# Storing each output tile by one DMA of 128 partitions in place of two of 64 (pooled attention, then a gated feed-forward layer)

## The chip, the core and the metric

The kernel runs on one core of a Trainium2 chip. The metric is the device time of one execution in microseconds (us). The engines are PE (TensorE), DVE (VectorE), ACT (ScalarE), POOL (GpSimd) and SP (SyncE), which only issues DMAs; a core has 16 DMA engines, which all queues share.

## The reference

Eight batches, eight heads, 576 positions, head size 64. Keys and values are averaged over runs of eight positions, so each head attends to 72 keys. The result, 512 wide, goes through a feed-forward layer with a convolution over three positions as gate.

```python
k_p = k.reshape(B, H, 72, 8, 64).mean(axis=3)
v_p = v.reshape(B, H, 72, 8, 64).mean(axis=3)
attn = softmax(q @ k_p^T / 8)
x = (attn @ v_p).transpose(0, 2, 1, 3).reshape(8, 576, 512)
h = relu(x @ w_in)                        # 512 -> 1024
gate = sigmoid(conv_w[0]*h[s-1] + conv_w[1]*h[s] + conv_w[2]*h[s+1])
out = (h * gate) @ w_out                  # 1024 -> 512, float32
```

## The kernel before, in words

The batches go in four pairs, the groups g = 0 to 3. The 1152 positions of a pair are cut into nine tiles t of 128 rows. A position s of a batch is written as s = 9p + c, with p from 0 to 63 and c from 0 to 8; a tile holds two blocks, and a block is the 64 rows p of one c of one batch. Tile 4 of a group holds the last block of its first batch and the first block of its second; each other tile holds two neighbouring values of c. That makes 36 output tiles.

For each tile of attention PE makes scores, DVE and ACT the softmax, and PE the values. From the third group on (`TURN_DMA = 2`) the softmax weights `e` are turned into `eT`, and the attention's result `x` into `xT`, by transposing DMAs on SP's queue (`att_send`, line 703, and `att_turn_out`, line 756); two larger ones turn `q` into `qT` (line 555). The feed-forward layer works a batch at a time: w_in (line 777), ReLU on ACT (line 786), the convolution on PE or on DVE (lines 941 and 913), the product with the gate on DVE (line 991).

The output of a tile: `ffn_out` (line 999) multiplies with w_out into a PSUM bank, `ffn_copy` (line 1010) copies the bank on ACT or DVE into a tile in SBUF of 128 partitions with 512 float32 each, and `ffn_store` (line 1022) writes it to the result, a row of 2 KB from each partition. Rows of a block lie nine rows (18,432 bytes) apart in the result. The SBUF tiles come from a ring of five, `osb`; the nine tiles of the last group come from a ring of their own of eleven, `late`, which is laid over old buffers and so has the names `qp` and `v` in the profile. A later writer of a buffer waits until the store that reads it has landed.

All stores of the first three groups are issued by SP, in one queue with the transposes; those of the last group by SP or ACT. The very last tile is made in two halves of 256 columns, each with its own copy and its own stores. The input loads are issued by POOL, but for the first ones.

The order of all instructions is written out in `ORDER`, a list of operations with the engine of each, and `PLACES`, the PSUM banks. An operation of that list may issue more than one instruction: the store of a tile is one operation that issues two DMAs, but for the last tile, where each of the four stores is an operation of its own (`only` says which block). The DMAs of SP and ACT count on eight semaphores in turn, so that one waits for the landing of the one that had its semaphore before.

Of the kernel before, what the change touches and what calls it, by code (L numbers as in the profile page):

```python
# [12 lines left out]
ACT = mybir.ActivationFunctionType  # L13
# [20 lines left out]
class Graph:  # L34
# [121 lines left out]
    def add(self, engines, key, emit, after=(), behind=(), uses=(), mode=None, land=None, count=10):  # L156
        o = Op(engines, key, emit, uses, mode, land, count)
        for a, started in [(x, False) for x in after] + [(x, True) for x in behind]:
            if a is not None:
                a.next.append((o, started))  # L160
                o.left += 1
        self.ops.append(o)
        return o
# [20 lines left out]
def kernel(  # L184
# [10 lines left out]
    nc = tc.nc  # L195
# [4 lines left out]
    d_model, d_ff = moe_w_in.shape  # L200
    P = 128
    C = 9
    TB = S // C
# [59 lines left out]
    def buf(*key):  # L263
        return buffers[key[0]][tokens[key].slots[0]]
# [728 lines left out]
    def half_columns(x):  # L993
        return slice(x * d_model // 2, (x + 1) * d_model // 2)

    def ffn_out(g, t, fbs, ps, columns=slice(0, d_model)):
        rows = P
        for fb in fbs:
            nc.tensor.matmul(  # L999
                out=bank(ps)[0:rows, columns],  # L1000
                lhsT=buf("gT", g)[:, fb, t * P:t * P + rows],
                rhs=w_out_sb[:, fb, columns],
                start=(fb == 0),
                stop=(fb == n_fb - 1),
            )

    def ffn_copy(g, t, ps, copy, columns=slice(0, d_model)):
        rows = P
        osb = buf("late" if g == 3 else "osb", g, t)
        copy(out=osb[0:rows, columns], in_=bank(ps)[0:rows, columns])  # L1010

    def ffn_store(g, t, queue, only=None, columns=slice(0, d_model)):
        osb = buf("late" if g == 3 else "osb", g, t)
        if t == 4:
            blocks = [(groups[g][0], C - 1), (groups[g][1], 0)]
        elif t < 4:
            blocks = [(groups[g][0], 2 * t), (groups[g][0], 2 * t + 1)]
        else:
            blocks = [(groups[g][1], 2 * t - 9), (groups[g][1], 2 * t - 8)]
        for j, (b, c) in enumerate(blocks):  # L1020
            if only in (None, j):
                queue.dma_start(
                    out=out[b].rearrange("(p c) d -> c p d", c=C)[c, :, columns],
                    in_=osb[j * TB:(j + 1) * TB, columns],
                )

    def pe(*columns):
        return {"PE": sum(n / 2400 + 0.0025 for n in columns)}  # L1030
# [7 lines left out]
    def either(d, a):  # L1038
        return {"DVE": d - 0.085, "ACT": a - 0.085}

    def copier(o):
        return nc.scalar.copy if o.engine == "ACT" else nc.vector.tensor_copy

    def token(ring, *key, n=1):
        t = tokens[(ring,) + key] = Token(ring, n)
        return t
# [11 lines left out]
    def nudge(kind, b):  # L1058
        return 0.0
# [49 lines left out]
    for n in range(Graph.SPARES):  # L1109
        t = token("ps")  # L1110
# [299 lines left out]
    def add_out(b, w):  # L1410
        w += nudge("o", b)
        g, i = where[b]
        rounds = (1, 3, 5, 6, 7)
        for n, t in enumerate(n_outs[b]):
            key = w + 3 * rounds[n] - 1 + Graph.OUT + (Graph.LAST if b == B - 2 else 0) if b < B - 1 else w + n
            key += nudge("ot", 9 * g + t)
            osb, free = (token("late", g, t), [x for n in range(4, B) for x in qdone[n, 0] + [vdone[n]]]) if g == 3 else (token("osb", g, t), [])
            need = [a for x in groups[g][0:i + 1] for a in gdone[x]]
            if b == B - 1 and n == len(n_outs[b]) - 1:
                o = None  # L1420
                for x in range(2):
                    sm = token("ps")
                    o = add(pe(*[P * 2] * 8), key + x, lambda t=t, x=x, sm=sm: ffn_out(g, t, range(n_fb), sm, half_columns(x)),
                            after=need + [wout, o], uses=[sm, gtok[g]], mode=FULL, count=16)
                    c = add(either(0.42, 0.38), key + x, None, after=[o] + free, uses=[osb, sm])
                    c.emit = lambda c=c, t=t, x=x, sm=sm: ffn_copy(g, t, sm, copier(c), half_columns(x))
                    for r in range(2):
                        c2 = add({"SP": 0.7, "ACT": 0.6}, key + x, None, after=[c], uses=[osb], land=(2.4, 0, 1))
                        c2.emit = lambda c2=c2, t=t, x=x, r=r: ffn_store(
                            g, t, nc.scalar if c2.engine == "ACT" else nc.sync, r, half_columns(x))  # L1430
                continue
            sm = token("ps")
            o = None
            for j in range(2):
                o = add(pe(*[512] * 4), key, lambda t=t, j=j, sm=sm: ffn_out(g, t, range(4 * j, 4 * j + 4), sm), after=need + [wout, o],
                        uses=[sm, gtok[g]], mode=FULL, count=8)
            o = add(either(0.69, 0.585), key, None, after=[o] + free, uses=[osb, sm])
            o.emit = lambda o=o, t=t, sm=sm: ffn_copy(g, t, sm, copier(o))
            o = add({"SP": 1.36, "ACT": 1.16} if g == 3 else {"SP": 1.36}, key, None, after=[o], uses=[osb], land=(2.4, 0, 1))
            o.emit = lambda o=o, t=t: ffn_store(g, t, nc.scalar if o.engine == "ACT" else nc.sync)  # L1440
# [10 lines left out]
    for b in range(B):  # L1451
        g, i = where[b]
        w = b * SLOTS
        add_ffn(b, w)
        if b + 1 < B:
            ng, ni = where[b + 1]
            ts = n_tiles[b + 1]
            gap = Graph.SPREAD / len(ts)
            for n, t in enumerate(ts):
                add_att(ng, t, w + Graph.ATT + n * gap)  # L1460
        add_out(b, w + SLOTS)
# [39 lines left out]
```

## Time and profile before

| what | value |
|---|---|
| time, median of 3 runs | 210.96 us (210.22 to 211.09) |
| the profiled execution's own time | 211.08 us |
| its span, first to last instruction | 209.2 us |
| mean granted TensorE clock | 0.993 |
| DMA: packets, bytes | 48,835 packets, 33.48 MB |
| HBM written | 9.44 MB, the whole result |

The span is what the views of the profile divide up; the profiled execution's own time is 1.9 us longer. A view of the DMA in a stretch of time gives the mean busy share of the 16 DMA engines in forty slices, the GB/s that they moved, and for each queue its packets and the time that these took, as a share of 16 engines over that stretch. Queue q0 is POOL's, q1 is SP's, q10 is ACT's. A row of data makes a packet of its size, and packets of 4 bytes mark the end of a DMA on each engine that worked on it.

### The profile page before, as it was taken

To read this page: it belongs to the slowest core of one execution; us is meant where nothing else is said; L and a number is where in the kernel's file an instruction comes from. 1 tells how busy PE (TensorE), PEld (TensorE's weight loads), DVE (VectorE), ACT (ScalarE), POOL (GpSimd) and SP (SyncE) were. 2 spreads that over 40 slices of the span, in tenths; PEclk is the share of its full clock that TensorE was granted. 3 is DMA by queue.
4 is the path that set the end of the run, shared out by engine and by line. 5 is a ranking of instruction groups with operands and counts; after the bars stand their busy time and mean duration, and the time that the engine had idled before them with its cause. 6 is when DMAs were issued, how large, how long until landed. Compare 5 with 4: busy or idle time off the path is not lost.

```text
span 209.2 us, 6541 instructions
## 1 busy us (share of the span) xinstructions
PE 197.5 (94%) x2650; PEld 134.5 (64%) x2666; DVE 190.2 (91%) x338; ACT 174.5 (83%) x363; POOL 45.4 (22%) x74
## 2 busy tenths in 40 slices
PE   4899999999999999999999999999999999999990
PEld 1468688776688887666867875566556666644450
DVE  7969999889999999999999999999999999999440
ACT  3558786998899999998998999999999999797310
POOL 8553034010173121010000152040234306000000
PEclk9999999999999999999999999999999999999997
DMA  5999999999999999998495975895665557044496
GB/s 189 251 204 207 207 207 208 210 205 205 189 151 195 207 209 206 179 155 169 89 147 97 120 126 122 110 134 130 137 138 123 116 126 174 0 100 102 107 270 179
DMA packets 48835, 33.48 MB, mean 160 GB/s; under 512 B 28300, under 2 KB 43812, under 8 KB 48804
## 3 DMA queue, kind: packets, MB, share of 16 engines
q0 software_dynamic: 15216, 15.40, 44.8%
q1 hardware_dynamic: 32592, 16.20, 38.7%
q10 hardware_dynamic: 996, 1.45, 2.8%
q8 instruction: 21, 0.34, 0.6%
q14 instruction: 10, 0.08, 0.2%
HBM read 32.52 MB, written 9.44 MB: 201 GB/s over the span
## 4 chain that ended last, share of the span: by engine, by line
PE 50%; DVE 24%; ACT 15%; issue 5%; DMA 3%; SPq 0%; DVEq 0%; ACTq 0%
PE psum L777 21%; PE psum L999 12%; DVE tg L913 6%; DVE negm L635 4%; ACT x L740 4%; PE psum L719 3%; DMA hT<-in_k_dram 3%; DVE gT L991 3%; DVE sd L647 3%; PE psum L941 2%; PE psum L694 2%; PE psum L609 2%; ACT hT L786 2%; ACT qT L561 2%; PE psum L764 1%
## 5 line engine op out<-in xcount | busy, mean ns | idle before, releaser
L777 PE MATMUL psum<-xT,w_in_sb 128*128 128x288 bf16 x512 | 70.6, 286 | 0.4
L999 PE MATMUL psum<-w_out_sb,gT 128*128 128x512 bf16 (+1 forms) x280 | 65.9, 373 | 1.1 <-issue 0.2
L777 PEld LDWEIGHTS <-w_in_sb 128*128 128x128 bf16 x512 | 48.3, 98 | 15.6 <-issue 0.6
L786 ACT ACTIVATE hT<-psum 128x576 bf16<-128x576 f32 x64 | 41.6, 671 | 4.8 <-PE psum L777 4.2
L999 PEld LDWEIGHTS <-gT 128*128 128x128 bf16 x296 | 27.7, 98 | 27.5 <-DVE gT L991 0.6
L861 POOL COPY hT<-hT 128x126 bf16<-128x126 bf16 x14 | 11.3, 809 | 84.2 <-issue 43.6
L913 DVE SCALAR_TENSOR_TENSOR tg<-hT,ratio 128x576 f32<-128x576 bf16 x36 | 28.2, 811 | 0.5 <-ACT gT L923 0.2
L635 DVE TENSOR_REDUCE negm<-psum 128x8 f32<-128x576 f32 (+2 forms) x37 | 27.3, 747 | 1.3 <-PE psum L609 0.7
L913 DVE SCALAR_TENSOR_TENSOR tg<-hT,ratio,tg 128x576 f32<-128x576 bf16 x36 | 28.1, 807 | 0.0
L923 ACT ACTIVATE gT<-tg,ratio 128x576 bf16<-128x576 f32 x36 | 27.3, 792 | 0.8 <-DVE tg L913 0.7
L991 DVE TENSOR_TENSOR gT<-gT,hT 128x2304 bf16<-128x2304 bf16 x16 | 21.4, 1348 | 0.1
L740 ACT ACTIVATE x<-psum,r 128x64 bf16<-128x64 f32 x96 | 21.2, 357 | 0.1
L1010 ACT COPY osb<-psum 128x512 f32<-128x512 f32 x27 | 16.4, 620 | 4.3 <-PE psum L999 2.7
L647 DVE TENSOR_TENSOR sd<-psum,negm 128x576 f32<-128x576 f32 x27 | 19.7, 745 | 0.1
L684 ACT ACTIVATE e<-sd 128x576 bf16<-128x576 f32 x27 | 19.4, 719 | 0.1
L719 PE MATMUL psum<-vm,eT 128*128 128x65 bf16 (+5 forms) x240 | 18.8, 222 | 0.2 <-DVE vm L517 0.2
L719 PEld LDWEIGHTS <-eT 128*128 128x128 bf16 (+1 forms) x240 | 14.8, 101 | 3.6 <-issue 0.8
L747 DVE TENSOR_TENSOR x<-psum,r 128x512 bf16<-128x512 f32 (+1 forms) x25 | 16.6, 678 | 0.2
L426 PE MATMUL psum<-gT 128*128 128x448 bf16 x40 | 13.0, 433 | 2.8 <-DVE gT L1108 2.8
L941 PE MATMUL psum<-hT,dw 64*64 64x63 bf16 (+2 forms) x448 | 13.2, 255 | 0.2 <-ACT kT L506 0.2
L513 DVE TENSOR_TENSOR v<-v 128x1280 bf16<-128x1280 bf16 (+2 forms) x24 | 12.9, 538 | 0.2
L941 PEld LDWEIGHTS <-dw 64*64 64x64 bf16 x448 | 10.9, 107 | 2.1 <-issue 1.4
(95 smaller groups left out, 236.5 us busy)
## 6 DMA issues: line engine op xcount, KB each, us to landing
out_dram<-osb SPq DMA_DIRECT2D x54, 128.0 KB, 2.4
v<-in_v_dram POOLq DMA_DIRECT2D x8, 512.0 KB, 13.9
qp<-in_q_dram POOLq DMA_DIRECT2D x7, 576.0 KB, 13.3
kk<-in_k_dram POOLq DMA_DIRECT2D x3, 1152.0 KB, 14.4
out_dram<-qp ACTq DMA_DIRECT2D x10, 128.0 KB, 3.3
hT<-in_k_dram SPq DMA_DIRECT2D x2, 576.0 KB, 5.3
w_in_sb<-in_moe_w_in_dram POOLq DMA_DIRECT2D x2, 512.0 KB, 15.3
w_out_sb<-in_moe_w_out_dram POOLq DMA_DIRECT2D x1, 1024.0 KB, 17.9
```

The lines of the kernel that those rows point to most:

```text
L635: nc.vector.tensor_reduce(out=a["m"][0:rows], in_=a["s"][0:rows, :, 0:2 * KW].rearrange("p a (h s) -> p a h s", s=Sp), axis=AX.X, op=OP.ma ...
L647: nc.vector.tensor_tensor(out=a["d"][0:rows], in0=a["s"][0:rows, :, 0:2 * KW].rearrange("p a (h s) -> p a h s", s=Sp), in1=a["m"][0:rows]. ...
L684: nc.scalar.activation(out=dst, in_=src, func=ACT.Exp,)
L719: nc.tensor.matmul(out=a["o"][lo:hi, h // 4, (h % 4) * (D + 1):(h % 4 + x1 - x0) * (D + 1)], lhsT=a["eT"][:, j, lo:hi], rhs=buf("vm", b)[: ...
L740: nc.scalar.activation(out=a["x"][0:rows, n * D:(n + 1) * D], in_=ov[:, n // 4, n % 4, 0:D], func=ACT.Identity, scale=r[0:rows, n // 4, n ...
L777: nc.tensor.matmul(out=banks(ps)[:, j, 0:SC], lhsT=w_in_block(dc, fb), rhs=buf("xT", g)[:, dc, i * S + j * SC:i * S + (j + 1) * SC], start ...
L786: nc.scalar.activation(out=h_of(b)[:, fb].rearrange("p (a s) -> p a s", a=2), in_=banks(ps)[:, :, 0:SC], func=ACT.Relu, scale=1.0 if (b, f ...
L913: nc.vector.scalar_tensor_tensor(out=acc, in0=h, scalar=w, in1=acc if tap else mid, op0=OP.mult, op1=OP.add)
L923: nc.scalar.activation(out=gate, in_=acc_of(b, fb, ps), func=squash(b, fb), scale=ratio[:, 1, fb:fb + 1])
L941: nc.tensor.matmul(out=banks(pss[r ^ c])[c * D:(c + 1) * D, j, lo:hi], lhsT=dw[r * D:(r + 1) * D, tap * n_fb + fb, :], rhs=hT[r * D:(r + 1 ...
L991: nc.vector.tensor_tensor(out=gate, in0=gate, in1=h_of(b)[:, four], op=OP.mult)
L999: nc.tensor.matmul(out=bank(ps)[0:rows, columns], lhsT=buf("gT", g)[:, fb, t * P:t * P + rows], rhs=w_out_sb[:, fb, columns], start=(fb == 0),
```

## The change

`ffn_store` issues one DMA for a whole tile. Its source is all 128 partitions of the tile in SBUF. Its target is an access pattern put together by hand over the two blocks: the outermost dimension counts the two blocks, with the distance between them as step, the next one the 64 rows of a block, the last one the columns. In the last tile the operation for the first block of a half now stores both blocks, and that for the second issues nothing.

```diff
-    def ffn_store(g, t, queue, only=None, columns=slice(0, d_model)):
+    def ffn_store(g, t, queue, columns=slice(0, d_model)):
         osb = buf("late" if g == 3 else "osb", g, t)
...
-        for j, (b, c) in enumerate(blocks):
-            if only in (None, j):
-                queue.dma_start(
-                    out=out[b].rearrange("(p c) d -> c p d", c=C)[c, :, columns],
-                    in_=osb[j * TB:(j + 1) * TB, columns],
-                )
+        b, c = blocks[0]
+        to = out[b].rearrange("(p c) d -> c p d", c=C)[c:c + 1, :, columns]
+        last = out[blocks[1][0]].rearrange("(p c) d -> c p d", c=C)[blocks[1][1]:blocks[1][1] + 1, :, columns]
+        step = last.offset - to.offset
+        to = bass.AP(tensor=to.tensor, offset=to.offset, ap=[[step, 2], *[list(x) for x in to.ap[1:]]])
+        queue.dma_start(out=to, in_=osb[:, columns])
...
-                            g, t, nc.scalar if c2.engine == "ACT" else nc.sync, r, half_columns(x))
+                            g, t, nc.scalar if c2.engine == "ACT" else nc.sync, half_columns(x)) if r == 0 else None
```

The order of the instructions on PE, DVE and POOL stays as it was, and on SP and ACT each pair of stores becomes one at the place of the first. SP's queue, where the transposes of the third group begin, minus before and plus now; `eT`, `qT` and `xT` are targets of transposes, and the sizes are those of the target's access pattern:

```order
 L703 DMA_TRANSPOSE eT_106<-e_99 128x5x128
-L1022 DMA out_dram<-osb_123 64x512 x2
-L1022 DMA out_dram<-osb_124 64x512 x2
+L1025 DMA out_dram<-osb_123 2x64x512
+L1025 DMA out_dram<-osb_124 2x64x512
 L555 DMA_TRANSPOSE qT_79<-qp_76 128x18x128
-L1022 DMA out_dram<-osb_126 64x512 x2
+L1025 DMA out_dram<-osb_126 2x64x512
 L756 DMA_TRANSPOSE xT_114<-x_107 128x4x128
 L703 DMA_TRANSPOSE eT_104<-e_103 128x5x128
```

Nothing changes its place; four issues between the transposes into `eT` and into `qT` become two, and the leading count of the target goes from 64 to 2.

The end of ACT's queue, where the last tiles of the last group are copied out of PSUM (`qp_77`, `v_87` are buffers of `late`) and stored:

```order
 L1010 COPY qp_77<-psum 128x512
-L1022 DMA out_dram<-qp_77 64x512 x2
-L1022 DMA out_dram<-v_87 64x256 x2
-L1496 UNCONDITIONAL_BRANCH
+L1025 DMA out_dram<-qp_77 2x64x512
+L1025 DMA out_dram<-v_87 2x64x256
+L1494 UNCONDITIONAL_BRANCH
```

The last four issues of ACT become two. The two of `v_87` were the blocks of the last tile's second half.

## The prediction

> **What bounds the kernel now.** I read the page first: who is busy, how the DMA engines fare over time, and the chain that ended last.
>
> ```profile
> PE 197.5 (94%) x2650; PEld 134.5 (64%) x2666; DVE 190.2 (91%) x338; ACT 174.5 (83%) x363; POOL 45.4 (22%) x74
> DMA  5999999999999999998495975895665557044496
> PE 50%; DVE 24%; ACT 15%; issue 5%; DMA 3%; SPq 0%; DVEq 0%; ACTq 0%
> ```
>
> PE is busy for 94% of the span, and the chain runs through PE, DVE and ACT; DMA has 3% of it. So the kernel is bound by compute. But the DMA engines are full for the first 17 slices of 5.23 us, and half full after. Next I asked for busy time by stage, cut where SP's queue changes its work.
>
> ```profile
> 0.00:56.00 56.00, 51.57 (x956) 36.56 (x959) 49.44 (x114) 40.80 (x68) 17.14 (x30) 1.00 1.17 209
> 56.00:89.00 33.00, 32.76 (x574) 25.68 (x576) 32.43 (x60) 31.98 (x64) 9.36 (x18) 1.00 1.17 188
> 89.00:165.00 76.00, 74.89 (x928) 50.61 (x923) 75.39 (x123) 73.86 (x178) 14.16 (x22) 1.00 0.73 128
> 165.00:195.00 30.00, 29.69 (x176) 17.10 (x178) 29.81 (x39) 26.37 (x55) 4.71 (x4) 1.00 0.43 96
> 195.00:209.20 14.20, 8.62 (x48) 4.51 (x46) 3.16 (x6) 1.49 (x3) 0.00 (x0) 0.90 0.73 205
> ```
>
> The last two columns are the DMA share and GB/s: over 1 in the load stages (packets of one engine overlap there), then 0.73, 0.43, 0.73. The stores leave room, as long as all 16 engines carry them. When they are issued is in the timeline of SP's queue:
>
> ```profile
> 56.70 1.19 SPq L1022 DMA_DIRECT2D out_dram<-osb  x2
> 82.75 6.36 SPq L703 DMA_TRANSPOSE eT<-e  x3
> 89.15 3.00 SPq L1022 DMA_DIRECT2D out_dram<-osb  x4
> ...
> 164.36 4.93 SPq L756 DMA_TRANSPOSE xT<-x  x3
> 169.38 15.46 SPq L1022 DMA_DIRECT2D out_dram<-osb  x14
> ```
>
> One tile is stored at 56.7 us. The other 35 come from 89.15 us on, mixed with transposes until 169.3 us.
>
> **What the change removes.** The issues of line 1022, by the view of that line (min/median/max in ns):
>
> ```profile
> L1022 SPq DMA_DIRECT2D out_dram<-osb x54: 466/591/1724, 56.7 to 202.2; - x54
> L1022 ACTq DMA_DIRECT2D out_dram<-qp x10: 473/527/1108, 195.4 to 204.1; - x10
> L1022 SPq DMA_DIRECT2D out_dram<-qp x6: 467/620/929, 187.3 to 203.4; - x6
> L1022 SPq DMA_DIRECT2D out_dram<-v x2: 683/768/852, 204.3 to 205.1; - x2
> L1022 ACTq DMA_DIRECT2D out_dram<-v x2: 473/516/560, 205.4 to 206.0; - x2
> ```
>
> Of 74 issues 37 go. SP saves 31 of some 0.59 us, 18 us, and none of it is on the chain (SPq 0%). ACT saves 6 of 0.52 us, at the very end, where nothing computes any more. So the gain is bounded by the tail: below, under the rivals.
>
> **What it adds: fewer engines for each store.** How many engines share a DMA can be counted from its packets. Four stores alone, and the first 9 us with ACT's only load, of 24 rows:
>
> ```profile
> DMA packets 320, 0.52 MB, mean 131 GB/s; under 512 B 64, under 2 KB 64, under 8 KB 320
> q1 hardware_dynamic: 320, 0.52, 56.7%
> out_dram<-osb SPq DMA_DIRECT2D x4, 128.0 KB, 2.4
> ...
> q10 hardware_dynamic: 36, 0.01, 1.0%
> gT<-in_moe_conv_w_dram ACTq DMA_DIRECT2D x1, 12.0 KB
> ```
>
> Four stores (182.4 to 186.4 us) make 256 packets of data and 64 small ones: 16 end marks for each 64 rows. The load of 24 rows makes 36 packets: 24 of data and 12 marks. With 16 engines at hand it ran on 12, which divides 24 evenly. So the engines are given equal shares of a leading count: 16 for 64, 12 for 24. The new store leads with 128 in SBUF and with 2 in the result (the 2x64x512 of SP's new rows). No DMA of this trace has sides that lead with different counts. Either the count of the source decides, then it is 16 engines, or the two sides must be cut alike, then the 2 blocks can be shared by 2 engines at most. I take 2: an engine that walks one side must know where it stands on the other, and a cut of the 64 inner rows is not a cut of the leading count.
>
> [...]
>
> **Its price.** Each of two engines then moves 64 rows of 2 KB where each of 16 moved 8. The lone stores took 56.7% of 16 engines for 4 us, 36.3 us for 256 rows, so 142 ns a row with all 16 engines on the same 64 partitions. In the tail SP's and ACT's queues run together and rows go faster (196 to 207 us):
>
> ```profile
> DMA  0297998997998898999488997997999899999969
> GB/s 0 67 253 164 231 156 239 373 305 216 417 305 209 291 261 216 268 313 313 179 246 223 253 201 186 365 358 224 298 253 179 201 313 365 261 305 283 287 235 283
> DMA packets 1750, 2.78 MB, mean 252 GB/s; under 512 B 342, under 2 KB 468, under 8 KB 1748
> q10 hardware_dynamic: 858, 1.36, 49.9%
> q1 hardware_dynamic: 890, 1.39, 38.6%
> ```
>
> On average 252 GB/s at 88.5% busy, 17.8 GB/s an engine or 115 ns a row; in the best slices 365 and 417 GB/s, 22.8 and 26.1 an engine, or 90 and 79 ns. Two engines that have the path to themselves are nearest to the best slices: I take 84 ns, 5.4 us a tile, with 79 to 115 ns for the range and 142 as a rival. If packets of stores overlapped as those of loads do (1.17 busy), 84 would act as 72 ns, 4.6 us a tile: that is the low end.
>
> **What else those two engines carry.** The transposes use all 16. From 89 to 195 us:
>
> ```profile
> DMA packets 29069, 12.63 MB, mean 119 GB/s; under 512 B 25984, under 2 KB 25984, under 8 KB 29056
> xT<-x SPq DMA_TRANSPOSE x18, 2.5
> eT<-e SPq DMA_TRANSPOSE x16, 2.7
> ...
> q1 hardware_dynamic: 6688, 1.65, 73.7%
> ```
>
> 25,984 small packets are 1624 an engine (the stores' marks among them). The last row is 99 to 113 us, where SP issues transposes alone: 6688 packets took 73.7% of 16 engines for 14 us, 24.7 ns each. So an engine spends 1624 x 24.7 ns = 40 us on them. They are in one queue with the stores: a transpose behind a store now lands some 5 us later, and attention waits, then PE.
>
> **The sum.** On the two engines, from 89.15 us:
> 36 tiles x 5.4 us = 194.4 us (35 from there on, and one for the tile at 56.7 us, which pushes 5.4 us of loads behind it while the engines are full), 40 us for transposes, 1.8 us from the last row to landing (2.4 us less the 0.57 us that four rows take). Together 325.4 us, if the two engines never rest. They rest when SP, which works in order, waits for compute before a transpose. From 89 to 165 us it waited, in 18 rows of which these are the first and last:
>
> ```profile
> SPq L756 <- ACT osb L1010: 4.8, 4, 2.2
> ...
> SPq L703 <- PE psum L941: 0.3, 1, 0.3
> ```
>
> In all 34 us. Stores still under way cover much of that; I count a third, 11 us. The end: 336 us of span. After 169 us compute has 40 us left without a transpose, against 20 tiles or 108 us of stores, so compute no longer counts. With the 1.9 us by which the profiled execution (211.08) is longer than its span: 338 us. That execution is within 0.1% of the median, so nothing is corrected.
>
> **Rivals.**
> 1. All 16 engines still share a store (its 128 rows are cut). For it: 128 rows can be shared by 16 engines as evenly as 64. Against: the count of 12 above shows that equal parts of a count decide, and 2 is one of the counts. Then only the tail changes:
>
> ```profile
> 203.66 0.42 DVE L1010 COPY v<-psum 128x256 f32<-128x256 f32 x1 [0.45 <-PE psum L999]
> 203.59 1.12 ACTq L1022 DMA_DIRECT2D out_dram<-qp  x2
> 205.41 1.13 ACTq L1022 DMA_DIRECT2D out_dram<-v  x2
> ```
>
> The last copy ends at 204.1 us, its last store is issued at 206.0 (ACT is held up by its earlier stores). One issue less for each of the last two tiles on ACT is 0.5 to 1.1 us: 210.0 to 210.6 us, I take 210.2. It decides if the new stores show 16 marks each. [...]
>
> 2. Two engines, at 142 ns a row: 9.1 us a tile, 36 x 9.1 = 327.6, with 89.15, 40, 1.8, 11 and 1.9 us 471 us. For it: it is the price of most stores now. Against: the rows of the tail.
>
> 3. Two engines, and little of it seen, because compute goes on while stores fall behind: then the five `osb` buffers would have to hold. They hold 27 us of stores, and 81 us come between 89 and 165 us (15 tiles). The bandwidth bound stays in any case: low prices and transposes that overlap alike (34 us at 1.17) give 89.15 + 36 x 4.6 + 34 + 1.8 + 1.9 = 292 us.
>
> **How the numbers follow.** Two engines: 0.90, of it 0.80 for prices of 72 to 115 ns, 0.06 for the second rival and beyond, 0.04 for less than 285 us. The first rival: 0.10; with 0.5% (1.05 us), what a measurement of this kernel can tell from no change, that is 0.04 faster, 0.06 the same. At 115 ns: 36 x 7.4 + 89.15 + 40 + 1.8 + 11 + 1.9 = 410 us. The range 285 to 410 us holds 0.8. Slower by over 0.5%: 0.90.
>
> **What would show it.** Right: stores of 256 KB that land after some 7 us in place of 2.4; 37 x 2 end marks in place of 74 x 16, so 1110 fewer packets, 47,725; in the tail under 55 GB/s with a small DMA share; PE at about 60% of the span, waiting behind transposes and `osb`; SP's queue ending the chain by DMA. Wrong: 592 end marks (48,243 packets) and a tail as fast as now; or DMA rows near 142 ns. The weakest terms are the price of a row on two engines and the third of SP's waits.

## The result and the profile after

| | before | after |
|---|---|---|
| time, median | 210.88 us (210.22 to 211.09) | 326.95 us (326.27 to 327.43) |
| ratio | | 1.551 (95% interval 1.546 to 1.556) |
| span of the profiled execution | 209.2 us | 325.5 us |
| granted TensorE clock, mean | 0.993 | 0.84 |

The changed kernel takes 116 us more. The page of the profile after, in the lines that answer to those of before: busy time of the engines; granted clock and DMA share in forty slices of 8.1 us, and GB/s; packets; the chain that ended last, by engine and by line.

```profile
PE 213.7 (66%) x2650; PEld 139.7 (43%) x2666; DVE 191.4 (59%) x338; ACT 175.5 (54%) x363; POOL 40.1 (12%) x74
PEclk9999999999999899798699598589587869555555
DMA  7999999999998998869879959811111111111111
GB/s 235 193 208 206 210 205 201 170 205 208 142 79 62 110 159 61 109 76 81 94 64 66 110 64 77 52 30 53 51 45 36 51 54 51 51 51 51 51 51 39
DMA packets 47725, 33.48 MB, mean 103 GB/s; under 512 B 27190, under 2 KB 42702, under 8 KB 47694
...
DMA 45%; PE 16%; ACT 8%; SPq 5%; issue 5%; DVE 4%; ACTq 3%; DVEq 0%; POOLq 0%
DMA out_dram<-osb 17%; DMA eT<-e 10%; DMA v<-in_v_dram 9%; PE psum L777 5%; DMA qp<-in_q_dram 5%; PE psum L999 4%; DMA xT<-x 3%; SPq L1025 3%; ACTq L1025 3%; ACT x L740 2%; DMA hT<-in_k_dram 2%; PE psum L719 2%; ACT osb L1010 2%; SPq L756 1%; DVE negm L635 1%
```

No engine is full any more, and DMA, which had 3% of the chain, has 45%. In the last third the DMA engines show a share of 0.1 and 51 GB/s, but for a gap near 243 us: two engines of sixteen. The packets are 1110 fewer, so each of the 37 stores has 2 end marks where each of 74 had 16.

The eights and nines in the row of the DMA share before that are not sixteen engines at full work, since GB/s fell. The trace keeps start, duration and size of every packet. From 89.6 to 215.1 us the packets of 256 bytes, which are those of the transposes, took 58 ns in the mean, where the kernel before had 24; the median is 18 ns in both. So a part of them stood for long. The trace names no engine, so it isn't shown what they stood for; the likely reading is the part of their transpose on the two engines that stores held.

The timeline of SP's queue (start, duration, both in us) shows the two stages:

```profile
89.61 2.44 SPq L1025 DMA_DIRECT2D out_dram<-osb  x2
92.16 12.85 SPq L555 DMA_TRANSPOSE qT<-qp  x1
...
199.85 12.55 SPq L756 DMA_TRANSPOSE xT<-x  x3
215.12 30.10 SPq L1025 DMA_DIRECT2D out_dram<-osb  x7
...
296.85 9.98 SPq L1025 DMA_DIRECT2D out_dram<-v  x1
```

The stage with transposes, 89.15 to 169.3 us before, now ends at 212.4 us. The 20 tiles after it start at 215.1 us, where before they started at 169.4. Who waited, over the whole run (total, times, longest):

```profile
ACT osb L1010 <- DMA out_dram<-osb: 37.5, 8, 8.3
PEld L719 <- DMA eT<-e: 24.2, 6, 10.3
PE psum L719 <- DMA eT<-e: 22.2, 6, 10.0
PE psum L777 <- DMA xT<-x: 6.6, 1, 6.6
```

ACT waits for a free output buffer, PE for softmax weights that a transpose has still to turn. Both are behind stores. The waits for `eT` and `xT` all fall into the stage with transposes, and so do 9.8 of ACT's 37.5 us; the other 27.7 us come after it. Busy time of the engines over that stage and the rest, before and then after (the last three columns are granted clock, DMA share and GB/s):

```profile
89.15:169.30 80.15, 78.99 (x938) 53.07 (x932) 79.54 (x129) 77.88 (x190) 15.43 (x24) 1.00 0.71 126
169.30:209.20 39.90, 34.06 (x194) 19.00 (x195) 28.68 (x38) 23.68 (x44) 3.43 (x2) 0.96 0.53 136
...
89.60:215.10 125.50, 89.40 (x944) 56.88 (x940) 81.11 (x130) 78.94 (x190) 11.94 (x24) 0.86 0.89 83
215.10:325.50 110.40, 40.98 (x194) 20.89 (x195) 28.03 (x36) 23.48 (x44) 1.61 (x2) 0.68 0.13 48
```

The stage with transposes is 45 us longer, and PE, the first column of busy time, has 10 us more of work in it, at a granted clock of 0.86 in place of 1.00. No run tells what these 10 us by themselves cost. The DMA view of the stage without transposes (222 to 312 us) gives the price of a row:

```profile
DMA packets 2195, 4.45 MB, mean 49 GB/s; under 512 B 34, under 2 KB 34, under 8 KB 2192
q1 hardware_dynamic: 1605, 3.23, 9.4%
q10 hardware_dynamic: 587, 1.19, 3.4%
```

The two queues fill 12.8% of 16 engines, which is two engines (12.5%) and a little more, because packets overlap: by the packet records two were under way for 87.6% of these 90 us, three for 9.7%, and never more. 12.8% of 16 x 90 us, for 2158 rows, is 85 ns a row. By what was moved, 51 GB/s on two engines, a row comes every 80 ns.

### The profile page after: what moved, and what is told of

Read it like the earlier page. It is cut to its first block, busy times and chain, and to the rows that moved or that the text cites. A ratio compares the mean times of both kernels' runs of the same rounds, so it can differ in the third digit from the quotient of the medians.

```text
span 325.5 us, 6493 instructions
## 1 busy us (share of the span) xinstructions
PE 213.7 (66%) x2650; PEld 139.7 (43%) x2666; DVE 191.4 (59%) x338; ACT 175.5 (54%) x363; POOL 40.1 (12%) x74
## 4 chain that ended last, share of the span: by engine, by line
DMA 45%; PE 16%; ACT 8%; SPq 5%; issue 5%; DVE 4%; ACTq 3%; DVEq 0%; POOLq 0%
DMA out_dram<-osb 17%; DMA eT<-e 10%; DMA v<-in_v_dram 9%; PE psum L777 5%; DMA qp<-in_q_dram 5%; PE psum L999 4%; DMA xT<-x 3%; SPq L1025 3%; ACTq L1025 3%; ACT x L740 2%; DMA hT<-in_k_dram 2%; PE psum L719 2%; ACT osb L1010 2%; SPq L756 1%; DVE negm L635 1%
## 5 line engine op out<-in xcount | busy, mean ns | idle before, releaser
L777 PE MATMUL psum<-xT,w_in_sb 128*128 128x288 bf16 x512 | 76.8, 302 | 12.3 <-DMA xT<-x 6.6
L999 PE MATMUL psum<-w_out_sb,gT 128*128 128x512 bf16 (+1 forms) x280 | 74.8, 410 | 12.2 <-ACT osb L1010 5.7
L777 PEld LDWEIGHTS <-w_in_sb 128*128 128x128 bf16 x512 | 50.9, 103 | 31.2 <-issue 14.2
L999 PEld LDWEIGHTS <-gT 128*128 128x128 bf16 x296 | 29.9, 105 | 44.7 <-issue 16.4
L1010 ACT COPY osb<-psum 128x512 f32<-128x512 f32 x27 | 16.3, 603 | 42.4 <-DMA out_dram<-osb 37.5
L719 PE MATMUL psum<-vm,eT 128*128 128x65 bf16 (+5 forms) x240 | 19.8, 228 | 22.3 <-DMA eT<-e 22.2
L732 DVE RECIPROCAL r<-psum 128x8 f32<-128x8 f32 (+1 forms) x37 | 7.2, 200 | 32.7 <-PE psum L719 31.4
L861 POOL COPY hT<-hT 128x126 bf16<-128x126 bf16 x14 | 7.7, 546 | 134.1 <-issue 75.0
L941 PE MATMUL psum<-hT,dw 64*64 64x63 bf16 (+2 forms) x448 | 14.2, 263 | 5.9 <-ACT osb L1010 5.6
L941 PEld LDWEIGHTS <-dw 64*64 64x64 bf16 x448 | 11.6, 110 | 7.9 <-issue 7.1
L426 PE MATMUL psum<-gT 128*128 128x448 bf16 x40 | 12.0, 403 | 2.8 <-DVE gT L1106 2.8
## 6 DMA issues: line engine op xcount, KB each, us to landing
v<-in_v_dram POOLq DMA_DIRECT2D x8, 512.0 KB, 15.9
```

Source lines behind the costliest of these rows:

```text
L719: nc.tensor.matmul(out=a["o"][lo:hi, h // 4, (h % 4) * (D + 1):(h % 4 + x1 - x0) * (D + 1)], lhsT=a["eT"][:, j, lo:hi], rhs=buf("vm", b)[: ...
L777: nc.tensor.matmul(out=banks(ps)[:, j, 0:SC], lhsT=w_in_block(dc, fb), rhs=buf("xT", g)[:, dc, i * S + j * SC:i * S + (j + 1) * SC], start ...
L941: nc.tensor.matmul(out=banks(pss[r ^ c])[c * D:(c + 1) * D, j, lo:hi], lhsT=dw[r * D:(r + 1) * D, tap * n_fb + fb, :], rhs=hT[r * D:(r + 1 ...
L999: nc.tensor.matmul(out=bank(ps)[0:rows, columns], lhsT=buf("gT", g)[:, fb, t * P:t * P + rows], rhs=w_out_sb[:, fb, columns], start=(fb == 0),
```

## The experiments

The theory: the target's leading count sets how many engines share a store, and 36 tiles at 84 ns a row on the same two engines set the end. Rival A: one large DMA from a pattern of three levels is slow as such. Rival B: the time comes from transposes that land late, not from the amount on two engines. Experiments 1 to 4 write rows to other places of the result, so they measure and could not replace the kernel.

**1. Two DMAs, leading count 2.** The store of before, with the 64 rows of a block walked as 2 x 32.

```diff
-                queue.dma_start(
-                    out=out[b].rearrange("(p c) d -> c p d", c=C)[c, :, columns],
-                    in_=osb[j * TB:(j + 1) * TB, columns],
-                )
+                to = out[b].rearrange("(p c) d -> c p d", c=C)[c, :, columns]
+                step, (d, w) = to.ap[0][0], to.ap[1]
+                to = bass.AP(tensor=to.tensor, offset=to.offset, ap=[[step, 2], [2 * step, 32], [d, w]])
+                queue.dma_start(out=to, in_=osb[j * TB:(j + 1) * TB, columns])
```

> Two DMAs of 64 partitions a tile as before, but the target of each leads with a count of 2 (2x32x512; the rows of a block are written in another order). Theory (the leading count of the target sets how many engines share a store, and engines 0 and 1 then carry 64 rows a tile at 84 ns): as the changed kernel, 327 us, within 10, with 2 end marks for each of 74 stores (47,799 packets). Rival A (one DMA of 128 partitions from a pattern of three levels is slow as such): 211 us. Rival B (the time comes from transposes that land late, not from the amount on two engines): two stores of 32 rows an engine let transposes in between more often, 270 to 320 us.

Measured: 328.07 us (ratio 1.560, 1.555 to 1.565).

```profile
DMA packets 47799, 33.48 MB, mean 102 GB/s; under 512 B 27264, under 2 KB 42776, under 8 KB 47768
```

The number of end marks is that of two engines (2 for each of 74 stores); that they are engines 0 and 1 is not shown, since the trace names none. Two DMAs of 64 partitions are as slow as the one of 128 as soon as the target leads with 2, so rival A is out as far as it is the size of the DMA. The three levels of the pattern are still here; experiments 2 and 3 have three levels too, and are far faster, so these are not what costs. Out as well is the form of rival B that expected less than 320 us.

**2. Two DMAs, leading count 4.** The same edit with `[[step, 4], [4 * step, 16], [d, w]]`.

> Two DMAs of 64 partitions a tile, each with a target that leads with 4 (4x16x512; rows of a block in another order). Theory: four engines with 32 rows a tile at 84 ns, 2.7 us; 36 x 2.7 = 97 us with 29 to 40 us of transposes from 89 us on, 217 to 230 us with landing and the 1.9 us outside the span, and up to 10 more where SP waits: 217 to 240 us. Rival A: 211 us. Rival B (late transposes): half of the changed kernel's delay, about 269 us.

Measured: 250.24 us (ratio 1.190, 1.186 to 1.193), between the two. SP's queue at the end of the transposes:

```profile
178.14 5.49 SPq L756 DMA_TRANSPOSE xT<-x  x3
184.17 19.99 SPq L1025 DMA_DIRECT2D out_dram<-osb  x14
```

Here neither side was right alone. The stage with transposes ends at 183.6 us, 14 us later than before, though its stores and transposes are only 70 to 81 us of work for four engines in its 95 us (15 tiles at 2.7 us, and 29 to 40 us). That part is rival B: transposes behind stores land late. The other part is bandwidth: 20 tiles x 2.7 us from 184.2 us on is 238 us, where compute without a transpose needed 40 us. My expectation had counted all tiles from 89 us and so missed that the last 20 can't start before the transposes are through. With landing and the time outside the span that makes 242 us. The DMA share from 184.1 to 249 us shows where the other 8 us went:

```profile
DMA  2222222222012222222122222222222222222210
```

Four engines would be 0.25, and there are gaps. By the packet records the rows took 93 ns in the mean here, 5.4 us more than 84 ns over 20 tiles, and for 4.1 us before the last row no store moved. The longest gap, at 200.4 us, ends after a copy for which ACT had waited for a free buffer. Why a row took 93 ns isn't shown.

**3. Two DMAs, leading count 8.** The same with `[[step, 8], [8 * step, 8], [d, w]]`.

> Two DMAs of 64 partitions a tile, each with a target that leads with 8 (8x8x512; rows of a block in another order). Theory: eight engines with 16 rows a tile, 1.3 to 2.3 us; 36 x 2.3 + 40 us from 89 us on is at most 212 us, so the engines hardly bind and compute does: 210 to 215 us. Rival B (late transposes): a quarter of the delay, about 240 us.

Measured: 218.05 us (ratio 1.037, 1.034 to 1.039), 3 us above the expected range. The transposes end at 169.1 us, as before, so what is left is the tail:

```profile
196.83 9.36 ACTq L1025 DMA_DIRECT2D out_dram<-qp  x6
206.29 0.59 ACT L1010 COPY qp<-psum 128x512 f32<-128x512 f32 x1 [8.95 <-DMA out_dram<-qp]
```

The same stores in the timeline of the kernel before:

```profile
196.93 5.95 ACTq L1022 DMA_DIRECT2D out_dram<-qp  x6
```

ACT, which works in order, takes 9.4 us for six stores of the last group and the waits between them, where it took 5.95, and copies the next tile after them. The two queues from 196 to 216 us:

```profile
q10 hardware_dynamic: 864, 1.44, 24.9%
q1 hardware_dynamic: 864, 1.44, 21.9%
```

Together 46.8% of 16 engines is nearly all of eight (50%). So eight engines do bind the kernel, but only at its end.

**4. One DMA of 128 partitions into a target that leads with 128.**

```diff
-        b, c = blocks[0]
...
+        rows = out[groups[g][0]:groups[g][1] + 1].rearrange("b s d -> (b s) d").rearrange("(p c) d -> c p d", c=C)
+        to = rows[t, :, columns]
         queue.dma_start(out=to, in_=osb[:, columns])
```

> One DMA of 128 partitions a tile as in the change, but into 128 evenly spaced rows of the result, so that its target leads with 128 (128x512; the rows of a tile go to other places of the pair's two batches, each row of the result is written once). Theory: 16 engines, 16 end marks for each of 37 stores (48,243 packets), and what the merging of issues is worth by itself: 209.5 to 211.0 us. Rows read from all 128 partitions take nearer 84 than 142 ns. Rival A (one large DMA is slow as such): over 250 us.

Measured: 207.87 us against 210.56 (ratio 0.988, 0.987 to 0.990): faster by 2.7 us, more than expected. The page's packets, then two of its stores alone (181 to 186 us), then the end of the timeline:

```profile
DMA packets 48243, 33.48 MB, mean 162 GB/s; under 512 B 27708, under 2 KB 43220, under 8 KB 48212
...
DMA packets 288, 0.52 MB, mean 105 GB/s; under 512 B 32, under 2 KB 32, under 8 KB 288
q1 hardware_dynamic: 288, 0.52, 28.0%
out_dram<-osb SPq DMA_DIRECT2D x2, 256.0 KB, 2.2
...
202.99 0.42 DVE L1010 COPY v<-psum 128x256 f32<-128x256 f32 x1 [0.45 <-PE psum L999]
203.44 0.34 ACTq L1016 DMA_DIRECT2D out_dram<-v  x1
```

There are 592 end marks, 16 for each of 37 stores: with 128 on both sides a store of 128 rows does run on 16 engines. 256 rows took 28.0% of 16 engines for 5 us, 87.5 ns a row, where stores of 64 partitions took 142. Neither 64 partitions nor 16 engines are slow by themselves: with two, four or eight engines on 64 partitions (experiments 1 to 3) the median row took 84 ns by the packet records (with eight, one in ten took some 160), and here, with 16 engines on 128, it took 86; only both together took 146. Why rows from 64 partitions cost 1.6 times as much on 16 engines (142 against 87.5 ns) isn't shown. The last store is issued 0.03 us after its copy. Before, ACT's last two stores, at 205.4 and 206.0 us, were one block of the last tile's first half and one of its second (not both of the second, as said with the change), and they were issued 2.2 and 1.9 us after the copies that they needed. Now the span ends 2.7 us after the last copy (before: 5.1). So merging as such is worth 1.2%; the change lost it with the leading count.

**5. The change in the last group alone.** `ffn_store` with the new store where `g == 3`, else the old ones.

> The change in the last group alone (9 of 36 tiles by one DMA that leads with 2; the others as before). No transposes run any more. Theory: the first such store is issued at about 187 us, 9 x 5.4 = 48.6 us on two engines, landing and the time outside the span: 187.3 + 48.6 + 1.8 + 1.9 = 239.6 us, within 4. Rival B (late transposes are what costs): 211 us.

Measured: 244.42 us (ratio 1.162, 1.156 to 1.168), 0.8 us above the stated margin. From 212 to 238 us the two queues fill two engines:

```profile
q10 hardware_dynamic: 432, 0.87, 8.6%
q1 hardware_dynamic: 295, 0.45, 4.6%
```

No transpose is left there, and still 34 us are lost, so the amount on two engines costs by itself. The 4 tiles in `osb` that SP still stores on 16 engines after 189 us had been left out; at 8 rows x 142 ns each they put 4.5 us on the same two engines, which brings 239.6 to 244.1. By the packet records some store was under way at every moment from 187.9 to 241.0 us.

**6. The change in the first three groups alone.** The same with `g < 3`.

> The change in the first three groups alone (27 of 36 tiles; the last group by two DMAs on 16 engines). Theory: the stage with transposes ends at 215 us as in the changed kernel, then 11 tiles x 5.4 us remain on the two engines, and the last group's 9 tiles on 16 engines add 0.7 to 1.1 us each there: 215 + 59.4 + 8 + 1.8 + 1.9 = 286 us, within 6. Rival B: nearly all of the delay, over 310 us.

Measured: 290.98 us (ratio 1.383, 1.371 to 1.396), within the margin. With experiment 5 the parts add up to the whole: 80.7 and 34.2 us are 114.9, against 116.1. An amount on two engines would add up like this, but so would any two delays one behind the other.

**7. The same stores from POOL's queue.** `nc.gpsimd.dma_start(out=to, in_=osb[:, columns])`.

> The changed kernel's stores, issued by POOL's queue in place of SP's and ACT's. Theory with engines that are always the same two: 315 us or more. If POOL's descriptors go to other engines for each store (the packets of all stores spread), the two-engine bound is gone, and what is left is a store's landing after some 7 us and POOL's queue, in order with its copies: 212 to 250 us. The DMA share in the tail tells: 0.12 with two engines, more if several stores move at once.

Measured: 282.20 us (ratio 1.341, 1.331 to 1.352), between both expectations. The end of it (240 to 279.8 us):

```profile
DMA  5223222114325446567578767696677684321000
GB/s 109 66 55 85 62 66 74 62 49 73 48 59 75 84 121 166 128 142 133 88 141 174 191 163 118 88 97 71 91 149 179 114 110 39 50 62 62 1 0 8
out_dram<-qp POOLq DMA_DIRECT2D x7, 256.0 KB, 17.0
```

Up to 191 GB/s, and a DMA share of up to 0.8, are more than two engines carry (51 GB/s and 0.13 in the changed kernel), so stores of this queue do move on different engines at the same time. But each took some 17 us to land there. And the transposes, alone in SP's queue now, end nearly as late as in the changed kernel, at 209.4 us against 212.4:

```profile
199.44 9.94 SPq L756 DMA_TRANSPOSE xT<-x  x3
```

PE still waits 15.9 us for `eT`. So the stage with transposes can be nearly as late without two engines that are always the same, and without stores ahead in the same queue. What is shown for the amount on two engines is the stage after it, by experiment 5 and by the DMA view of the changed kernel. Which of the two, landing or POOL's order, holds the kernel at 282 us was not separated.

**8 and 9. Stores of the last group on POOL's queue,** to get the faster tail of experiment 4 with the rows in their places. The kernel before, with `nc.gpsimd if o.engine == "ACT"` in place of `nc.scalar`, and then `nc.gpsimd if g == 3`, for the first eight tiles of the group.

> The kernel before (two DMAs of 64 partitions a tile), but the last group's stores that ACT issued go to POOL's queue, except those of the last tile. Theory (the last stores start late because they wait in the queues and for the semaphores of the stores before them; the kernel with one DMA of 128 rows ended 2.7 us after its last copy, the kernel before 5.1 us): with ten DMAs less on the eight semaphores the last two stores start within 0.3 us of their copies: 208.3 to 210.0 us. Rival (POOL's stores land late, as in the run with all stores on POOL, 8 us and more): 210.5 to 213 us.

> As the run before, but all stores of the last group's first eight tiles go to POOL's queue, SP's too. Theory: one queue issues 16 DMAs in some 11 us, 0.8 us each, so its last one starts 2 us or more after its copy and lands late: 210.5 to 214 us. If POOL keeps up, as the run before: 208.3 to 210 us.

Measured: 211.06 us (ratio 1.0023, 1.0012 to 1.0035) and 210.57 us (1.0007, 0.9992 to 1.0021). The end of the first of them:

```profile
203.41 1.40 ACTq L1022 DMA_DIRECT2D out_dram<-v  x2
203.82 0.42 DVE L1010 COPY v<-psum 128x256 f32<-128x256 f32 x1 [0.45 <-PE psum L999]
204.63 1.86 SPq L1022 DMA_DIRECT2D out_dram<-v  x2
```

Each of the two pairs is one block of the first half and one of the second. ACT's pair starts at 203.4 us in place of 205.4, but SP's at 204.6 in place of 204.3, and takes 1.86 us. The last issue ends at 206.5 us in both kernels, and the span is 209.6 us: no gain. So no version was found that keeps each row in its place and beats the kernel before.

## Why the prediction was right, step by step

- **Two engines for a store that leads with 2**: right, and shown by the end marks. 37 x 2, 74 x 2, 74 x 4, 74 x 8 and 37 x 16 marks give the packets of the changed kernel and of experiments 1 to 4 to the last one. In these runs a store whose sides lead with different counts (128 and 2; 64 and 2, 4, 8) left as many marks as the smaller count. Why the smaller one decides isn't shown: that an engine which walks one side must know where it stands on the other was my reasoning.
- **84 ns a row, 5.4 us a tile**: right, 85 ns by the share and 80 by what was moved. From the first of the last 20 tiles to the end are 110.4 us, where the sum has 108 and 1.8. That it fits to 0.6 us is luck: by the packet records stores were under way for 105.8 us, 5.3 a tile, and for 3.2 us before the last row nothing moved, which the sum had at nothing. The reason given for 84, two engines with the path to themselves, is not the whole of it, since 16 engines had 87.5 ns from 128 partitions.
- **Transposes and rests**: over-sized. From 89.61 to 215.12 us are 125.5 us, where the sum has 137: 16 tiles (15 are issued here, the other is the one at 56 us), 40 us of transposes and 11 us of rests. This is the whole difference between 338 and 327. By the packet records stores were under way for 83.6 of the 125.5 us, and nothing moved for 9.5, so the rests were sized well (the longest are shown below). At most 32 us are left for transposes alone, and the loads behind the tile at 56 us ended 3.6 us later than before, not 5.4. Whether a transpose is cheaper on these two engines than 24.7 ns a packet, or runs beside a store, stays open, because the trace doesn't tell engines apart.
- **Transposes land late**: right, and not only with two engines. Experiment 2 shows 14 us of it where bandwidth was not yet the limit of that stage, and in experiment 7 the stage ends nearly as late with stores on changing engines. The sum got that stage as an amount on two engines, and the size came out about right; that the amount is what held it is not shown.
- **PE at about 60%**: 66%, since its busy time rose from 197.5 to 213.7 us as the granted clock fell to 0.84. A landing of 7 us couldn't be read: the profile gives none for these stores. The sign that SP's queue would end the chain did not come: 45% of the chain is DMA, but its last piece is a copy on ACT at 282.9 us.
- **Rival 1** fell, but its gain, 0.5 to 1.1 us, was sized too low. Experiment 4 has it at 2.7 us. It took ACT's saved issues to come when nothing computes any more, but four of the six are issued while PE still multiplies, which it does until 203.6 us. It counted issues alone, and missed that rows leave faster from 128 partitions (87.5 against 142 ns), so that the last stores no longer wait for those before them.
- **Rival 2** (142 ns a row) fell with the 85 ns, and **rival 3** with the waits for `osb`, 37.5 us in all.

The rests at the end of the stage with transposes, as the row of the DMA share from 207 to 216 us shows them; its zeros are the waits of SP before the last transpose and before the stores of the last 20 tiles:

```profile
DMA  1111199900000000000000008981000000000000
```

## What to carry to other kernels

Look at the leading count of both sides of a DMA before merging transfers: on the queues of SP and ACT a store whose target led with 2 ran on two engines, the ones of 64 partitions as well as those of 128 (2 end marks each, 328.07 and 326.95 us). The end marks in the packet count told how many engines a store of these queues ran on: 2, 4, 8 or 16. A transpose left 32 (256 for the eight from 99 to 113.3 us of the kernel before), so its marks can't be read that way. Lead with the rows (207.87 us with 128), or keep two DMAs (210.88 us).

## What the runs showed of the hardware that I had not expected

An issue was not free late in the changed kernel. By the view of line 1025 (min/median/max in ns) a store that took 0.51 us to issue held its queue for up to 10 us near the end:

```profile
L1025 SPq DMA_DIRECT2D out_dram<-osb x27: 511/512/10048, 56.1 to 276.6; - x27
L1025 ACTq DMA_DIRECT2D out_dram<-qp x5: 534/2503/10053, 261.8 to 283.5; - x5
```

10 us is near twice a tile's 5.4 us, the pace of either queue when SP and ACT share the two engines. That the issue waits for the engines is read from this pace; the trace doesn't show it directly. On ACT this stops the copies that stand behind the store: one that started to issue at 272.8 us took 10.05 us, and the next copy starts at 282.9.
